# Gate and value products of a gated layer in pairs of groups and of f blocks, two of three k blocks by a scheme of seven products

## The chip, the cores and the metric

One core of a Trainium2 chip runs the whole program. Its engines run side by side, each through its own queue in order: TensorE (PE; its weight loads are listed as PEld), VectorE (DVE), ScalarE (ACT), GpSimd (POOL), and SyncE (SP), which here issues nearly all DMAs. The metric is device time in microseconds (us).

## What is computed

A delta-rule attention writes 3072 tokens x 384 features, and two feed-forward layers follow. The change is in the second, which takes the first's result `x` (3072 x 384) with 1536 hidden features (f):

```python
def _moe2_ref(x, w_gate, w_val, w_out):
    gate = 1.0 / (1.0 + np.exp(-(x @ w_gate)))
    val = x @ w_val
    return (gate * val @ w_out).astype(np.float32)
```

All is float32. A number is kept as two parts in a reduced format, a high part and the rest ("lo", the number minus its high part), and each matrix product is three: high x high, lo weight x high input, high weight x lo input.

## The kernel before

The tokens stand in six groups of 512 (`GT`, group index g), the 1536 hidden features in twelve blocks of 128 (`NF2`, index f), the 384 input features in three k blocks (`KD`). Values are laid out with features on partitions and the 512 tokens of a group in the free dimension, so a matmul is 128 x 128 weights against 128 x 512 inputs, written to one bank of PSUM (there are eight).

All instructions are recorded in the order in which they shall stand (`manual_schedule`). Attention and most of the first layer follow a table of tokens, `ORDER`; the last group of the first layer and the whole second layer are plain loops, at the end of the kernel function. In the first layer's last group (line 828) step n issues the hidden product `moe1_h`, the loads of the next weight rests from DRAM on SP (`fetch_low`), the output product `moe1_o` of step n - 2 and VectorE's rest `moe1_g`; between them stand the loads and splits of the second layer's weights (`w2_load`, `w2_split`), the making of float weights from raw 64-bit numbers (`w2_late`, steps of `narrow`) and of the first input (`load_x2`, `split_x2`).

The second layer runs over n = (g, f) from line 947. `moe2_h` makes the gate and the value sum of one block: 9 matmuls each (3 k blocks x 3 parts) into a tile `gv`, of which there are four. ScalarE takes the sigmoid of the first (`sg`), VectorE multiplies it with the second (`p`), ScalarE makes its high part (`ph`), VectorE its rest (`pl`). Then `moe2_o` of n - 1 stands on TensorE: the second product of the block before, 9 matmuls (3 output blocks x 3 parts) added up over f in three banks `o0` to `o2`. After a group's last f VectorE transposes the three banks and SP writes them out. In the last group the second product is turned round (`ph` and `pl` are the weights, 384 columns), 12 matmuls per f into four banks, and needs no transpose.

## Time and profile before

| | |
|---|---|
| median of three runs | 1099.5 us (1098.2 to 1100.1) |
| profiled execution: device time, span | 1103.99 us, 1102.3 us |
| mean granted TensorE clock | 0.98 |
| busy share of the span: PE, PEld, DVE, ACT, POOL | 93%, 78%, 53%, 39%, 14% |
| share of TensorE in the chain that ended last | 87% |

The span runs from the first to the last instruction. The busy share is a mean over very different stretches: attention and first layer up to 653 us, second layer after that. What a change in the second layer does is read there. A matmul's duration in a row is its latency; the next one starts before it has ended, so the pace is read from the distance of starts. Where an instruction sat idle before it started, the row names what ended the wait.

### The profile page before, as it was taken

The page shows a single profiled execution, that of the slowest core. Times are in us where ns is not written, and L with a number is a line of the kernel's source. Part 1 is how long each engine was busy: PE and PEld are TensorE (multiplying, and loading weights), DVE is VectorE, ACT ScalarE, POOL GpSimd, SP SyncE. Part 2 cuts the span into 40 slices and gives each one's busy share as a digit, 9 for nine tenths or more (in the row PEclk, how much of TensorE's full clock was granted, in tenths as well). Part 3 has the DMA queues.
Part 4 walks back from the last instruction along what each step waited for, and adds up shares of the span by engine and source line. Part 5 has one row for each costly group of instructions (what it writes and reads, how often), then busy time and mean ns, then how long its engine had stood idle before and what let it go on. Part 6 is the DMA issues. An engine that isn't in the chain of part 4 may idle for free.

```text
span 1102.3 us, 26935 instructions
## 1 busy us (share of the span) xinstructions
PE 1030.3 (93%) x11719; PEld 854.8 (78%) x11719; DVE 581.5 (53%) x1099; ACT 429.5 (39%) x688; POOL 150.0 (14%) x117
## 2 busy tenths in 40 slices
PE   3576999989999999999997999999999999999997
PEld 2474788878887888888885888888888888888886
DVE  6779889858777776775232357532222222322221
ACT  2253665544463555455444564312212112122111
POOL 4352454101001101010100020300001001000000
PEclk9998999999998999999997999999999999999999
DMA  9766667675774956665555652101020010010101
GB/s 242 193 208 166 214 209 203 195 189 145 211 200 144 232 159 193 184 167 174 135 169 154 202 199 94 43 20 38 1 58 1 4 55 1 20 38 1 29 1 29
DMA packets 93030, 135.56 MB, mean 123 GB/s; under 512 B 45552, under 2 KB 72304, under 8 KB 92400
## 3 DMA queue, kind: packets, MB, share of 16 engines
q1 hardware_dynamic: 92624, 133.57, 42.4%
q8 instruction: 92, 1.51, 0.6%
q10 hardware_dynamic: 288, 0.26, 0.1%
q14 instruction: 26, 0.21, 0.1%
HBM read 108.63 MB, written 20.45 MB: 117 GB/s over the span
## 4 chain that ended last, share of the span: by engine, by line
PE 87%; DVE 5%; DMA 3%; issue 3%; ACT 1%; SPq 1%; POOL 0%; DVEq 0%; ACTq 0%; POOLq 0%
PE gv L867 27%; PE h L665 17%; PE o L703 17%; PE o L893 11%; PE o L929 2%; PE att L582 2%; PE att L539 1%; PE att L524 1%; PE att L351 1%; PE att L570 1%; DMA il<-w1d 1%; PE att L552 1%; DMA kn<-in_kn_dram 1%; PE att L604 1%; DVE tt L440 1%
## 5 line engine op out<-in xcount | busy, mean ns | idle before, releaser
L875 DVE TENSOR_TENSOR p<-sg,gv 128x512 f32<-128x512 f32 x72 | 49.5, 687 | 252.9 <-PE gv L867 252.9
L679 ACT ACTIVATE gg<-h 128x512 f32<-128x512 f32 x96 | 57.4, 598 | 198.2 <-PE h L665 193.2
L688 DVE TENSOR_TENSOR gl<-gg,gh 128x512 fp32r<-128x512 f32 x96 | 72.3, 759 | 102.0 <-ACT gg L682 101.7
L867 PE MATMUL gv<-xhi,w2h 128*128 128x512 f32 x432 | 121.5, 389 | 0.0
L867 PE MATMUL gv<-xlo,w2h 128*128 128x512 f32 x432 | 121.4, 389 | 0.0
L867 PE MATMUL gv<-xhi,w2l 128*128 128x512 f32 x432 | 121.4, 389 | 0.0
L703 PE MATMUL o<-gh,il 128*128 128x512 f32 x288 | 113.2, 393 | 5.7 <-DMA il<-w1d 5.7
L873 ACT ACTIVATE sg<-gv 128x512 f32<-128x512 f32 x72 | 43.0, 597 | 172.0 <-PE gv L867 172.0
L877 ACT CAST ph<-p 128x512 fp32r<-128x512 f32 x72 | 44.6, 620 | 157.3 <-DVE p L875 157.3
L867 PEld LDWEIGHTS gv<-xlo,w2h 128*128 128x128 f32 x432 | 81.1, 188 | 17.0
L867 PEld LDWEIGHTS gv<-xhi,w2l 128*128 128x128 f32 x432 | 81.1, 188 | 17.0
L867 PEld LDWEIGHTS gv<-xhi,w2h 128*128 128x128 f32 x432 | 80.9, 188 | 16.2
L703 PE MATMUL o<-gh,w1h 128*128 128x512 f32 x216 | 87.6, 405 | 0.0
L665 PE MATMUL h<-xhi,il 128*128 128x512 f32 x288 | 84.7, 403 | 2.1 <-issue 1.7
L703 PE MATMUL o<-gl,w1h 128*128 128x512 f32 x216 | 85.1, 394 | 0.0
L879 DVE TENSOR_TENSOR pl<-p,ph 128x512 fp32r<-128x512 f32 x72 | 50.6, 703 | 49.4 <-ACT ph L877 49.4
L116 POOL TENSOR_TENSOR xlo<-x2r,xhi 128x512 fp32r<-128x512 f32 x18 | 24.7, 1370 | 335.5 <-ACT xhi L115 335.5
L893 PE MATMUL o<-ph,w2h 128*128 128x512 f32 x180 | 70.0, 389 | 0.0
L893 PE MATMUL o<-ph,w2l 128*128 128x512 f32 x180 | 70.0, 389 | 0.0
L893 PE MATMUL o<-pl,w2h 128*128 128x512 f32 x180 | 70.0, 389 | 0.0
L665 PE MATMUL h<-xhi,w1h 128*128 128x512 f32 x216 | 66.3, 417 | 1.9 <-ACT gg L679 1.9
L665 PEld LDWEIGHTS h<-xhi,il 128*128 128x128 f32 x288 | 55.9, 195 | 15.2 <-issue 2.2
(142 smaller groups left out, 1845.6 us busy)
## 6 DMA issues: line engine op xcount, KB each, us to landing
il<-w1d SPq DMA_DIRECT2D x192, 192.0 KB, 3.6
raw<-in_w_dram SPq DMA_DIRECT2D x19, 768.0 KB, 4.8
w1s<-in_w_dram SPq DMA_DIRECT2D x9, 768.0 KB, 5.1
w1d<-wl SPq DMA_DIRECT2D x16, 384.0 KB, 4.1
kz<-in_kz_dram SPq DMA_DIRECT2D x32, 192.0 KB, 5.2
kn<-in_kn_dram SPq DMA_DIRECT2D x12, 384.0 KB, 4.6
kt<-in_kq_dram SPq DMA_DIRECT2D x24, 192.0 KB, 5.2
q<-in_kq_dram SPq DMA_DIRECT2D x24, 192.0 KB, 5.2
```

The source lines that it names most:

```text
L116: eng.tensor_tensor(out=dst_lo, in0=src, in1=dst_hi.bitcast(F32), op=ALU.subtract)
L582: nc.tensor.matmul(out=psv[c][tok(a), k, :], lhsT=k2_t[st][tok(a), 8 * c + k, :], rhs=u_t[st][tok(a), 8 * c + k, 0:HD], start=True, stop=True,
L665: nc.tensor.matmul(out=ps[:, cs], lhsT=w[:, kc * 128:kc * 128 + 128], rhs=x[:, kc, cs], start=(i == 0 and kc == 0), stop=(i == 2 and kc == ...
L679: nc.scalar.activation(out=gg, in_=ps, func=ACTF.Relu)
L688: nc.vector.tensor_tensor(out=gl, in0=gg, in1=gh.bitcast(F32), op=ALU.subtract)
L703: nc.tensor.matmul(out=po[m], lhsT=w[:, cs], rhs=x, start=(f == 0 and i == 0), stop=(f == NF1 - 1 and i == 2),)
L867: nc.tensor.matmul(out=ps, lhsT=w[:, kc * 128:kc * 128 + 128], rhs=x[:, kc, :], start=(i == 0 and kc == 0), stop=(i == 2 and kc == KD - 1),)
L873: nc.scalar.activation(out=sg, in_=pss[0], func=ACTF.Sigmoid)
L875: nc.vector.tensor_tensor(out=p, in0=sg, in1=pss[1], op=ALU.mult)
L877: nc.scalar.copy(out=ph, in_=p)
L879: nc.vector.tensor_tensor(out=pl, in0=p, in1=ph.bitcast(F32), op=ALU.subtract)
L893: nc.tensor.matmul(out=po2[m], lhsT=w[:, m * 128:m * 128 + 128], rhs=x, start=(f == 0 and i == 0), stop=(f == NF2 - 1 and i == 2),)
```

## The change

The loop over (g, f) goes. Groups are taken in pairs and f blocks in pairs, so a step has four sums to make: A, B, C, D for two groups x two f blocks, first for the gate, then for the value. One such step for the gate or the value is a half in what follows; there are 36 (3 pairs of groups x 6 pairs of f blocks x 2).

Of the three k blocks, two form with the two groups and the two f blocks a product of 2 x 2 block matrices. It is made with seven block products of sums and differences of the weights (`w_sums`) and of the inputs (`x_sum`) in place of eight. The third k block takes four products as before (`K11` to `K22`). With three parts each that is 33 matmuls in a half. They stand in seven pieces (`PIECES`) of one or two block products, each piece with a PSUM bank of its own, `gx` and `gy` in turn. The first is copied by ScalarE into a tile in SBUF, every later one is added by VectorE to one or two of the tiles A to D, seven adds in a half. When a sum is complete (`DONE`) the sigmoid (gate) or the product with the gate (value) is made in place in SBUF, and then high part and rest as before.

The second product is issued in small portions between pieces (`FILL`: 3, 2, 2, 3, 2, 3 and 3 matmuls after the seven pieces), from a queue that is filled after each value half. Two groups are summed up at a time, so six banks hold the second product and two the pieces. In halves 0 and 1, where the queue is empty, and in the last nine halves, where only one group needs banks (the portions are `FILL_END` there), the pieces have five banks. The last group's second product comes at the very end, one output block of 36 matmuls after another.

Weights are made once, in the first pair of groups: ScalarE's high parts, VectorE's sums, GpSimd's rests; they are stored to DRAM (`w_keep`, 1.2 MB a half) and fetched again two halves ahead in the later pairs (`w_fetch`). Sums, high parts and rests of the inputs of the next pair are made by ScalarE and GpSimd during the pair before; those of the first pair by ScalarE and VectorE in the last group of the first layer, where the splits of before stood. Weights of the last four f blocks are made from raw numbers in twelve slabs of 384, seven in the first layer's last group and five in halves 2 to 6. Tiles of the first layer move to a pool of their own; the table `ORDER` is the same.

TensorE, in the middle of the second layer, before (`gv` the gate or value sum, `o` the second product; w2h and w2l are high part and rest of the weights):

```order
L867 MATMUL gv<-xhi,w2l_8993 128x512 x3
L867 MATMUL gv<-xlo,w2h_8992 128x512 x3
L893 MATMUL o_9601<-ph,w2h_8990 128x512 [waits Activation_49]
L893 MATMUL o_9601<-ph,w2l_8991 128x512
L893 MATMUL o_9601<-pl,w2h_8990 128x512 [waits DVE_49]
L893 MATMUL o_9602<-ph,w2h_8990 128x512
```

The same of the changed kernel (`gx` and `gy` the two banks of the pieces, `xb` input sums, `wg` weights, `wo` output weights):

```order
L1135 MATMUL gx<-xb,wg 128x512 [waits DVE_49]
L1135 MATMUL gx<-xb,wg 128x512 x5
L1014 MATMUL o_10499<-gh,wo 128x512
L1014 MATMUL o_10499<-gl,wo 128x512
L1014 MATMUL o_10472<-p_10774,wo 128x512
L1135 MATMUL gy<-xb,wg 128x512 [waits DVE_49]
L1135 MATMUL gy<-xb,wg 128x512 x2
L1014 MATMUL o_10472<-p_10774,wo 128x512
L1014 MATMUL o_10472<-p_10775,wo 128x512
```

The 9 matmuls of a second product are spread over four pieces, and nearly every piece begins with a wait for VectorE.

VectorE in the second layer before, where a group ends:

```order
L875 TENSOR_TENSOR p<-sg,gv 128x512 [waits PE_49,Activation_49]
L879 TENSOR_TENSOR pl<-p,ph 128x512 [waits Activation_49]
L901 STREAM_TRANSPOSE obt<-o_10094 128x16x32 [waits DMAHW4_49,DMAHW3_49,DMAHW5_49,DMAHW2_49,DMAHW6_49,DMAHW1_49,DMAHW7_49,DMAHW0_49,PE_49]
L901 STREAM_TRANSPOSE obt<-o_10095 128x16x32 [waits PE_49]
L901 STREAM_TRANSPOSE obt<-o_10096 128x16x32 [waits PE_49]
```

VectorE in a value half of the second pair of groups (L1047 are the adds from the piece's bank, L1058 the product with the gate, L1066 the rest):

```order
L1047 TENSOR_TENSOR valB<-valA,gx 128x512 [waits PE_49,Activation_49]
L1047 TENSOR_TENSOR valA<-valA,gy 128x512 [waits DVE_49,PE_49]
L1047 TENSOR_TENSOR valC<-valB,gx 128x512 [waits PE_49]
L1058 TENSOR_TENSOR valA<-gateA,valA 128x512 [waits DVE_49]
L1047 TENSOR_TENSOR valD<-valB,gy 128x512 [waits PE_49]
L1047 TENSOR_TENSOR valB<-valC,gy 128x512 [waits DVE_49]
L1047 TENSOR_TENSOR valC<-valC,gx 128x512 [waits DVE_49,PE_49]
L1066 TENSOR_TENSOR gl<-valA,gh 128x512 [waits Activation_49]
L1058 TENSOR_TENSOR valB<-gateB,valB 128x512
L1047 TENSOR_TENSOR valD<-valD,gy 128x512 [waits PE_49]
L1058 TENSOR_TENSOR valC<-gateC,valC 128x512 [waits DVE_49]
L1066 TENSOR_TENSOR gl<-valB,gh 128x512 [waits Activation_49]
```

Two operations per block have become eleven per half, and an add stands behind products and rests of the blocks before it.

VectorE in the first layer's last group before (gl is that layer's own rest, w2l the rest of second-layer weights):

```order
L116 TENSOR_TENSOR w2l_8492<-t,w2h_8491 128x1152 [waits DMAHW5_49,Activation_49]
L688 TENSOR_TENSOR gl<-gg,gh 128x512 [waits DVE_49,PE_49]
L688 TENSOR_TENSOR gl<-gg,gh 128x512 [waits DVE_49,PE_49,Activation_49]
L138 TENSOR_SCALAR y_8891<-raw_8786 128x1152 [waits DMAHW1_49,Activation_49]
L142 SCALAR_TENSOR_TENSOR raw_8786<-raw_8786,y_8891 128x1152 [waits DVE_49]
```

And of the changed kernel (L790 to L800 a slab, L910 and L922 sum and rest of an input, L868 rests of weights, L700 the layer's own rest):

```order
L868 TENSOR_TENSOR wg<-wr,wg 128x640 [waits Activation_49]
L700 TENSOR_TENSOR gl<-gg,gh 128x512 [waits PE_49,Activation_49]
L790 TENSOR_SCALAR y_8490<-raw_8489 128x384 [waits DMAHW5_49,DMAHW4_49,Activation_49]
L794 SCALAR_TENSOR_TENSOR raw_8489<-raw_8489,y_8490 128x384 [waits DVE_49]
L798 TENSOR_SCALAR y_8490<-raw_8489 128x384 [waits DVE_49]
L800 SCALAR_TENSOR_TENSOR raw_8489<-raw_8489,y_8490 128x384 [waits DVE_49]
L910 TENSOR_TENSOR xt<-x2r,xt 128x512
L922 TENSOR_TENSOR xlo<-x2r,xhi 128x512 [waits Activation_49]
L868 TENSOR_TENSOR wg<-wr,wg 128x512 [waits Activation_49]
```

Behind each of the layer's own rests stand seven operations here where two or three stood. The core of the diff:

```diff
-W2A, W2B = 6, 8
+W2A, W2B = 4, 8
+NP = NF2 // 2
+W_PLACE = dict(B2=0, B3=1, A1=2, A2=3, A3=4, S1=5, S2=6, S3=7, S4=8)
+X_PLACE = dict(P1=0, P6=1, P2=2, K1=3, P7=4, P5=5, P4=6, K2=7, P3=8, KD=9)
+UNITS = dict(
+    P1=("A1", "P1"), P6=("S2", "P6"), P2=("A2", "P2"), P7=("S3", "P7"), P5=("S1", "P5"), P4=("B2", "P4"),
+    P3=("S4", "P3"), K11=("A3", "K1"), K12=("A3", "K2"), K21=("B3", "KD"), K22=("B3", "K2"),
+)
+PIECES = ("P1", "P6", "P2 K11", "P7 K22", "P5", "P4 K21", "P3 K12")
+DONE = {2: ("A", 0, 1), 4: ("B", 1, 0), 5: ("C", 0, 0), 6: ("D", 1, 1)}
+FILL, FILL_END = (3, 2, 2, 3, 2, 3, 3), (2, 1, 1, 1, 1, 1, 2)
...
+        def w_sums(q):
+            t = raw_w[q]
+            b = [t[:, 128 * i:128 * i + 128] for i in range(10)]
+            for d, p, m, op in ((6, 0, 1, ALU.add), (7, 6, 3, ALU.subtract), (8, 3, 0, ALU.subtract), (9, 4, 7, ALU.subtract)):
+                nc.vector.tensor_tensor(out=b[d], in0=b[p], in1=b[m], op=op)
...
+        def w_low(q, i, eng=None):
+            a, b = (128 * x for x in PARTS[i])
+            h, t = ring_w[q][:, 0, a - 128:b - 128], ring_w[q][:, 1, a - 128:b - 128]
+            (eng or nc.vector).tensor_tensor(out=t, in0=raw_w[q][:, a:b], in1=h.bitcast(F32), op=ALU.subtract)
...
-        def moe2_h(n):
...
-            for v in range(2):
-                hi, lo = (w[:, v * DM:(v + 1) * DM] for w in w2_t[f])
-                ps = ps_2.tile([128, GT], F32, tag="gv", name="gv")
-                for i, (w, x) in enumerate([(hi, xh), (lo, xh), (hi, xl)]):
-                    for kc in range(KD):
...
+        def o_product(g, f, m, i, start, stop):
+            if start:
+                po2[g, m] = (
+                    ps_o.tile([128, GT], F32, tag=f"o{m}", name=f"o{m}") if g % 2 == 0
+                    else ps_2.tile([128, GT], F32, tag=f"o{m + 3}", name=f"o{m + 3}")
+                )
+            hi, lo = (w[:, m * 128:m * 128 + 128] for w in wo_t[f])
+            ph, pl = p_t[g, f]
+            w, x = ((hi, ph), (lo, ph), (hi, pl))[i]
+            nc.tensor.matmul(out=po2[g, m], lhsT=w, rhs=x, start=start, stop=stop)
...
+        def gate_done(t):
+            nc.scalar.activation(out=t, in_=t, func=ACTF.Sigmoid)
+        def val_done(t, sg, key):
+            nc.vector.tensor_tensor(out=t, in0=sg, in1=t, op=ALU.mult)
+            def high():
+                p_t[key] = p_tiles(key)
+                nc.scalar.copy(out=p_t[key][0], in_=t)
+            def low():
+                ph, pl = p_t[key]
+                (nc.gpsimd if key[0] in PLP else nc.vector).tensor_tensor(out=pl, in0=t, in1=ph.bitcast(F32), op=ALU.subtract)
+            later(PHD, high)
+            later(PLD, low)
...
+            if hh == 2:
+                p2.close()
+                ps_2 = ps_g = p2.enter_context(tc.tile_pool(name="ps_2", bufs=1, space=PSUM, reuse_waits="tile"))
...
+            if q < 2 * NP:
+                for k, i in enumerate((WP0, WP1)[v]):
+                    bg.setdefault(i, []).append((
+                        lambda: w_high(q, 0), lambda: w_sums(q), lambda: w_high(q, 1), lambda: w_low(q, 0, WLE[0]), lambda: w_low(q, 1, WLE[1])
+                    )[k])
...
+            for i, piece in enumerate(PIECES):
+                us = piece.split()
+                b = "xy"[step[0] % 2]
+                ps = ps_g.tile([128, GT], F32, tag=f"g{b}", name=f"g{b}", bufs=1 if 1 < hh < wide else {"x": 2, "y": 3}[b])
+                for u in us:
+                    wk, xk = UNITS[u]
+                    at_ = 128 * W_PLACE[wk]
+                    hi, lo = (w[:, h, at_:at_ + 128] for h in range(2))
+                    xh, xl = x[xk]
+                    for k, (a, c) in enumerate([(hi, xh), (lo, xh), (hi, xl)]):
                         nc.tensor.matmul(
-                            out=ps, lhsT=w[:, kc * 128:kc * 128 + 128], rhs=x[:, kc, :],
-                            start=(i == 0 and kc == 0), stop=(i == 2 and kc == KD - 1),
+                            out=ps, lhsT=a, rhs=c, start=k == 0 and u == us[0], stop=k == 2 and u == us[-1],
                         )
-                pss.append(ps)
-            sg = w2x.tile([128, GT], F32, tag="sg", name="sg")
-            nc.scalar.activation(out=sg, in_=pss[0], func=ACTF.Sigmoid)
-            p = work.tile([128, GT], F32, tag="gg", name="p")
-            nc.vector.tensor_tensor(out=p, in0=sg, in1=pss[1], op=ALU.mult)
-            ph = work.tile([128, GT], F32R, tag="gh", name="ph", bufs=3)
-            nc.scalar.copy(out=ph, in_=p)
-            pl = work.tile([128, GT], F32R, tag="gl", name="pl", bufs=3)
-            nc.vector.tensor_tensor(out=pl, in0=p, in1=ph.bitcast(F32), op=ALU.subtract)
-            p_t[n] = (ph, pl)
+                if i == 0:
+                    nc.scalar.copy(out=t["A"], in_=ps)
+                else:
+                    steps = ("BA", "AA", "CB", "DB BC", "CC", "DD")[i - 1].split()
+                    for d, a in steps:
+                        add(t[d], t[a], ps)
+                    if i in DONE:
+                        d, k, f = DONE[i]
+                        key = g0 + k, 2 * j + f
+                        if v == 0:
+                            later(GD, lambda d=t[d]: gate_done(d))
+                        else:
+                            later(VD[i], lambda d=t[d], sg=sgs[d], key=key: val_done(d, sg, key))
+                for fn in after.pop(step[0], ()):
+                    fn()
+                for fn in bg.pop(i, ()):
+                    fn()
+                for _ in range((FILL, FILL_END)[hh >= wide - 1][i]):
+                    if queue:
+                        one, end = queue.pop(0)
+                        one()
+                        if end is not None:
+                            closing(end)
+                for _ in range(3):
+                    if puts:
+                        puts.pop(0)()
+                step[0] += 1
...
+            if v:
+                assert not queue
+                for k, (g, f) in enumerate(((g0, fo), (g0, fe), (g0 + 1, fe), (g0 + 1, fo))[:4 if g0 + 2 < NG else 2]):
+                    for m in range(KD):
+                        for r in range(3):
+                            queue.append([
+                                lambda g=g, f=f, m=m, r=r, a=j == 0 and k % 2 == 0 and r == 0, z=j == NP - 1 and k % 2 and r == 2:
+                                o_product(g, f, m, r, bool(a), bool(z)), None])
+                    if j == NP - 1 and k % 2:
+                        queue[-1][1] = g
...
+        for m in range(4):
+            cs = slice(m * 128, m * 128 + 128)
+            po_m = ps_r.tile([128, DM], F32, tag=f"r{m}", name=f"r{m}")
+            for f in range(NF2):
+                hi, lo = wo_t[f]
+                ph, pl = p_t[NG - 1, f]
+                        out=po_m, lhsT=x[:, cs], rhs=w, start=f == 0 and i == 0, stop=f == NF2 - 1 and i == 2
```

## Rows read from the trace of the kernel before

**Rows 1.** Page: span, busy time with share and instructions.

```profile
span 1102.3 us, 26935 instructions
...
PE 1030.3 (93%) x11719; PEld 854.8 (78%) x11719; DVE 581.5 (53%) x1099; ACT 429.5 (39%) x688; POOL 150.0 (14%) x117
```

**Rows 2.** Windows: busy us of PE, PEld, DVE, ACT, POOL; clock, DMA, GB/s.

```profile
653.30:700.00 46.70, 46.70 (x208) 38.67 (x207) 28.22 (x31) 20.55 (x28) 7.12 (x4) 1.00 0.38 136
...
900.00:1000.00 100.00, 100.00 (x443) 82.82 (x442) 24.89 (x37) 23.05 (x39) 6.44 (x5) 1.00 0.06 16
```

**Rows 3.** Chain that ended last, in order of time: start us, us, what.

```profile
804.41 4.08 PE gv L867 x18
...
810.53 4.08 PE gv L867 x18
...
1091.08 4.28 PE o L929 x24
```

**Rows 4.** One line's instructions: duration ns min/median/max, first and last start us.

```profile
L867 PE MATMUL gv<-xhi,w2h x432: 389/389/398, 653.3 to 1089.3; 128*128 128x512 f32 x144
```

**Rows 5.** Timeline: start us, us, engine line op, idle before and what ended it.

```profile
1021.85 0.84 PE L867 MATMUL gv<-xlo,w2h 128*128 128x512 f32 x3
...
1022.80 0.69 DVE L875 TENSOR_TENSOR p<-sg,gv 128x512 f32<-128x512 f32 x1 [4.05 <-PE gv L867]
...
581.06 0.61 ACT L679 ACTIVATE gg<-h 128x512 f32<-128x512 f32 x1
...
581.72 0.96 PE L665 MATMUL h<-xhi,w1h 128*128 128x512 f32 x3 [1.85 <-ACT gg L679]
```

**Rows 6.** Three lines as in rows 4; then groups: busy us, mean ns.

```profile
L875 DVE TENSOR_TENSOR p<-sg,gv x72: 679/687/689, 657.6 to 1091.2; 128x512 f32<-128x512 f32 x72
...
L879 DVE TENSOR_TENSOR pl<-p,ph x72: 691/692/1503, 659.0 to 1092.6; 128x512 fp32r<-128x512 f32 x72
...
L591 DVE TENSOR_TENSOR state<-state,att x20: 540/547/555, 106.6 to 548.7; 128x384 f32<-128x384 f32 x20
...
L440 DVE TENSOR_TENSOR tt<-tt,tmp 128x126 f32<-128x126 f32 x4 | 1.2, 290 | 0.1
...
L151 DVE SCALAR_TENSOR_TENSOR w1s<-w1s,y 128x768 f32<-128x768 uint32 x9 | 8.6, 959 | 0.3
...
L138 DVE TENSOR_SCALAR y<-raw 128x768 uint32<-128x768 uint32 x12 | 6.6, 551 | 4.7 <-ACT raw L133 4.7
```

**Rows 7.** Timeline, VectorE alone, operations that don't wait for each other.

```profile
504.05 1.30 DVE L688 TENSOR_TENSOR gl<-gg,gh 128x512 fp32r<-128x512 f32 x2 [7.47 <-ACT gg L682]
```

**Rows 8.** Timeline, GpSimd and VectorE where they meet, then each alone.

```profile
701.51 1.37 POOL L116 TENSOR_TENSOR xlo<-x2r,xhi 128x512 fp32r<-128x512 f32 x1 [4.26 <-ACT xhi L115]
...
701.76 2.33 DVE L142 SCALAR_TENSOR_TENSOR raw<-raw,y 128x1152 uint32<-128x1152 uint32 x1
...
684.63 1.36 DVE L142 SCALAR_TENSOR_TENSOR raw<-raw,y 128x1152 uint32<-128x1152 uint32 x1
...
767.70 1.29 POOL L116 TENSOR_TENSOR xlo<-x2r,xhi 128x512 fp32r<-128x512 f32 x1 [55.52 <-ACT xhi L115]
```

**Rows 9.** Windows, a stretch of the first layer's last group.

```profile
620.00:640.00 20.00, 19.70 (x87) 15.97 (x87) 7.78 (x8) 12.51 (x20) 3.20 (x2) 1.00 0.75 258
```

**Rows 10.** Windows and timeline, the wait for weights at 585 us.

```profile
580.00:600.00 20.00, 12.59 (x38) 9.54 (x39) 6.71 (x9) 8.40 (x15) 1.47 (x1) 0.66 0.41 131
...
590.77 0.79 PE L703 MATMUL o<-gh,il 128*128 128x512 f32 x1 [5.69 <-DMA il<-w1d]
```

**Rows 11.** Timeline and DMA issues (x count, KB, us to landing) at the end.

```profile
1095.00 0.34 PE L929 MATMUL o<-w2h,pl 128*128 128x384 f32 x1
...
1095.38 0.56 DVE L938 COPY ob<-o 128x384 f32<-128x384 f32 x1 [0.49 <-PE o L929]
...
1094.29 5.04 SPq L944 DMA_DIRECT2D out_dram<-ob  x8
...
out_dram<-ob SPq DMA_DIRECT2D x8, 96.0 KB, 2.2
```

More of the change, by code (lines that the diff above doesn't have):

```diff
@@ L205, in rests @@
     def rests(f):
[L206 removed]
+        wl_t[f] = w1s.tile([128, 2 * DM], F32R, tag="wl", name="wl", bufs=1)
         nc.gpsimd.tensor_tensor(out=wl_t[f], in0=wt_t.pop(f), in1=w1h[f].bitcast(F32), op=ALU.subtract)
@@ L808 @@
[L808 to L819 removed]
+        NW, HS, SLAB, SST = 7, (2, 3, 4, 5, 6), (2, 3, 4, 6, 7, 8, 10), 4
@@ new lines, with x_high, x_low, x_steps @@
+        X_SAME = dict(P1=(0, 0), P2=(1, 0), P3=(1, 1), K1=(2, 0), K2=(2, 1))
+        def x_high(p, u):
+            if u in X_SAME:
+                k, g = X_SAME[u]
+                xt[u] = x2r_t[:, g, k]
+            nc.scalar.copy(out=x2[p][u][0], in_=xt[u])
+        def x_low(p, u, eng):
+            eng.tensor_tensor(out=x2[p][u][1], in0=xt[u], in1=x2[p][u][0].bitcast(F32), op=ALU.subtract)
+        X_ORDER = ("P5", "P1", "P6", "P2", "P4", "K1", "KD", "K2", "P7", "P3")
+        def x_steps(p, eng_s, eng_l):
+            def one(i):
+                if i == 0:
+                    open_x(p)
+                if i < len(X_ORDER) and X_ORDER[i] not in X_SAME:
+                    x_sum(X_ORDER[i], eng_s)
+                if i:
+                    x_high(p, X_ORDER[i - 1])
+                    x_low(p, X_ORDER[i - 1], eng_l)
+            return [lambda i=i: one(i) for i in range(len(X_ORDER) + 1)]
@@ L855 @@
[L855 to L866 removed]
+            for one in plan.get(n - N1 + NF1 - 2, ()):
+                one()
@@ new lines, with later, add, closing @@
+        after, queue, puts = {}, [], []
+        step = [0]
+        def later(k, fn):
+            after.setdefault(step[0] + k, []).append(fn)
+        def add(d, a, b, eng=None):
+            (eng or nc.vector).tensor_tensor(out=d, in0=a, in1=b, op=ALU.add)
+        def closing(g):
+            for m in range(KD):
+                later(1 + 2 * m, lambda m=m: turn(g, m))
+            later(6, lambda: puts.extend(put_out(g)))
+        def gate_done(t):
+            nc.scalar.activation(out=t, in_=t, func=ACTF.Sigmoid)
@@ new lines @@
+        while after:
+            k = min(after)
+            for fn in after.pop(k):
+                step[0] = k
+                fn()
+        for one, _ in queue:
+            one()
+        for m in range(KD):
+            turn(NG - 2, m)
+        puts = put_out(NG - 2)
+        p2.close()
+        ps_r = ctx.enter_context(tc.tile_pool(name="ps_r", bufs=1, space=PSUM, reuse_waits="tile"))
+        for m in range(4):
[4 more added lines that the diff above has]
+                ph, pl = p_t[NG - 1, f]
@@ new lines @@
+            ob = obt_t.rearrange("p a (b n) -> p (a b) n", b=2)[:, m]
+            o_out = ob.rearrange("p (q m i) -> p m q i", q=4, m=KD)
+            o_in = po_m.rearrange("p (m q i) -> p m q i", q=4, m=KD)
+            if m % 2:
+                nc.vector.tensor_copy(out=o_out, in_=o_in)
+            else:
+                nc.scalar.copy(out=o_out, in_=o_in)
+            for one in puts[16 * m:16 * m + 16]:
+                one()
+            s = 2 * (NG - 1) + m // 2
+            for b in range(2):
+                r0 = (2 * (m % 2) + b) * SEQ + s * C
+                nc.sync.dma_start(out=out[r0:r0 + C, :], in_=ob[64 * b:64 * b + 64])
```

367 lines of the change are left out of this document (223 added, 144 removed).

## The prediction

> **What bounds the kernel now.** I read the page first: the span is 1102.3 us and PE is busy for 93% of it [rows 1]. The windows then say where: from 653.3 us, when the second layer begins, to 1089 us TensorE has no pause at all at a granted clock of 1.00, while VectorE is busy 28.2 of the first 46.7 us and about a quarter of the time after that [rows 2]. The chain of waits there is nothing but TensorE: one f block of one group is 27 matmuls and comes round every 6.12 us, and the last 24 matmuls end the kernel [rows 3]. So a matmul of 512 columns costs 6.12 / 27 = 0.2267 us (its 389 ns in [rows 4] are its latency, not its pace), and in this stage a matmul that goes is time that goes, as long as TensorE is never kept waiting instead. Everything up to the last group of the first layer stands on every engine in the order of before, with the same waits, so the first 600 us stay.
>
> **What is removed.** Gate and value products go from 1296 matmuls (432 of each of three kinds, one of them in [rows 4]) to 1188: for two groups, two f blocks and one of gate or value ("a half" below) 33 stand where 36 stood. The second product keeps its 540 and 144. So 108 x 0.2267 = **24.5 us** go, all of it from the path.
>
> **What is added, in the steady state.** Before, a finished gate or value sum was read once, at leisure, out of four banks. Now each half has seven pieces of 3 or 6 matmuls in two banks in turn, ScalarE copies the first and VectorE adds the other six into SBUF with seven adds, and a piece can start only when the piece two before it has been read. Between pieces stand 2 or 3 matmuls of the second product (18 in a half), so a half takes 51 x 0.2267 = 11.56 us of TensorE. Prices: a read begins 0.50 us after the last matmul of a sum has begun (gate product at 1021.85 x3, the last at 1022.30, VectorE at 1022.80) [rows 5]. An add of SBUF and PSUM is of the kind of L875, 0.687 us; L591, the same form in 384 elements, never left 0.54 to 0.56 us [rows 6]. VectorE operations that don't depend on each other start 0.61 us apart (two of 512 in 1.30 us) [rows 7], dependent ones 0.72. TensorE resumes within 0.1 us of what it waited for (ScalarE ends at 581.67, TensorE starts at 581.72) [rows 5].
> Walk through a value half, time 0 at its start. Piece 3 (counted from 0) has its last matmul 24 intervals in: read from 24 x 0.2267 + 0.50 = 5.94 to 6.63; its bank is wanted by piece 5 at interval 33, 7.48. Spare 0.85. Piece 4 has two adds: 30 x 0.2267 + 0.50 = 7.30, two dependent adds to 8.71; wanted at interval 42, 9.52. Spare 0.81. The other pieces have 1.0 us or more. Over two halves VectorE has 14 adds, 4 products and 4 subtractions, 22 x 0.61 to 0.72 = 13.4 to 15.8 us against 23.1 us of TensorE. So in the second and third pair of groups I take the pieces as hidden; what covers them is the second product between pieces, and without it each would show.
>
> **What is added, in the first pair of groups.** Here weights and inputs are prepared as well. TensorE: two halves without second product (33 matmuls) and ten of 51, 576 x 0.2267 = 130.6 us. VectorE: 132 operations as above at 0.65, 86 us; 40 weight sums of 128x128 (0.29, the 128x126 row), 11.6; 12 rests of the output weights of 384 (0.55, as L591), 6.6; five slabs of late weights, each two fused operations and two shifts of 384, by the 768-element rows (0.96 and 0.55) scaled down about 1.8 together, 9.1 [rows 6]. Sum 113 us: 87%, against 66% later. Spare of 0.8 us no longer covers everything:
> - halves 0 and 1 have no second product between pieces. Half 1 wants 7 adds, 3 products, 1 subtraction, 4 sums and 2 rests, some 10 us, from VectorE in 7.5 us of TensorE, and then five banks shrink to two: 1.0 us late at half 2.
> - halves 2, 4 and 6: four sums (1.2) and a slab operation stand between the reads of piece 3 and piece 4: 5.94 + 0.69 + 1.2 + 0.56 + 1.41 = 9.8 against 9.52, with the backlog of the half before 0.5 each: 1.5.
> - halves 7 to 11: GpSimd makes the sums and rests of the next inputs there (below): 2.0.
> Later: 0.8 in the second pair for the same work of GpSimd, 0.5 for the transposes that fall on the two-bank pieces of the next group pair, and 0.7 at the end, where the last C block's rest (VectorE 12.7 us after the start of the last half, by the same walk) is wanted 12.0 us after it. The last group of the first layer: VectorE was busy 7.8 of 20 us there [rows 9]; per step of 4.08 us it now has a subtraction of 0.69, a slab of 1.8, an input sum and rest (1.3), in two steps weight sums and rests too (5.7 us in all), so it falls 2 us behind; its result is wanted two steps later. Late weights and their stores also stand on SP ahead of the first layer's weights, two steps after the work that they wait for. 1.0. What such a wait could cost is in the trace: 5.69 us once, for weights behind a store on SP [rows 10].
> Stalls: 1.0 + 1.5 + 2.0 + 0.8 + 0.5 + 0.7 + 1.0 = **7.5 us**, between 0 (every wait covered) and the rivals below. ScalarE's and GpSimd's own time, the store and reload of the prepared weights (1.2 MB a half, 102 GB/s) and SP hide: the stage moved 16 GB/s [rows 2] where the group before it moved 258 [rows 9], no ring is wanted within 11 us of its fetch, and output DMAs go three to a piece.
>
> **The end.** Before, four output blocks finish together: the last matmul starts at 1095.00, SP issues eight DMAs until 1099.33, landing takes 2.2 us, the span ends 7.3 us after that matmul [rows 11]. Now the blocks finish one after another, 36 matmuls apart. After the last one stand a copy (1095.38 + 0.56, so 0.94 after the matmul), two issues of 0.63, 2.2 of landing and the 0.8 us that remain before too: 5.2. **2.1 us** less.
>
> **Sum.** 24.5 + 2.1 - 7.5 = 19.1 us less. The profiled execution took 1103.99 us around its span of 1102.3; the three timed runs have a median of 1099.5. The difference carries over: 1099.5 - 19.1 = **1080.4 us**.
>
> **Rivals.**
> *VectorE and GpSimd hold each other up, and VectorE becomes the bound in the first pair.* GpSimd's subtraction at 701.51 took 1.37 us, and VectorE's operation of 701.76, which reads two SBUF operands, took 2.33 us where the same line takes 1.36 at 684.63: it ended 1.21 us after GpSimd, most of an operation. Subtractions of L879 range from 0.69 to 1.50, reads from PSUM (L875, L591) never move [rows 6, 8]. In the first pair GpSimd now has 20 weight rests (1.6 and 1.3 us), five slab sums (0.8) and 15 input operations (1.29), some 52 us, scaled from [rows 8]. If half of that falls on VectorE's products, rests and sums, it has 26 us more against 17.6 spare. TensorE then waits 8.4 us if all of the spare lies where it is wanted, 17 if half does, in place of the 4.5 that I counted: 1084 to 1093 us. For it: VectorE's order is dense there. Against it: 84 of its 132 operations of the steady kind are adds from PSUM, and GpSimd is free to run where TensorE and VectorE are at others. The Trainium skill, "SBUF — State Buffer", section "Who interferes with whom", states this as a rule that speaks against the change: a VectorE instruction with two SBUF inputs and a GpSimd instruction that reads SBUF exclude each other, and whoever comes second waits the other one out; the trace agrees (0.97 us more of 1.36).
> *Two banks are too few, and it gets slower.* The place is the piece boundary, 175 of them in the 25 halves that have two banks. It decides when reads end later than my walk by more than the spare of 0.8 us: then every 0.1 us costs 17.5 us, and 0.26 us eat up all of the gain. An add that takes 1.4 us in place of 0.69 (in place in SBUF, as no row of before has it in 512) would put piece 4 0.6 us over and VectorE at 24 us of work per 23.1: at least 25 x 0.6 + 18 x 1 = 33 us more, 1113 us. Against it: L591 has exactly this form and a steady time.
> *No stall at all*: 26.6 us less, 1073.
>
> **How the numbers follow.** Forecast (1075 to 1086): 0.61. Contention beyond it (1086 to 1093 and a little more): 0.22. No stalls: 0.06. Stalls that eat it up to within 0.2% (2.2 us): 0.03. Slower: 0.08. 0.2% is about what a measurement of this kernel can tell from no change. Faster 0.89, same 0.03, slower 0.08. The range leaves out the slower rival and the tips: 1073 to 1094.
>
> **What would show it.** The second layer's matmuls 108 fewer, still 0.2267 us apart; waits of TensorE on VectorE nearly all in the first 130 us of the stage, under 2 us each; GpSimd's time in that stretch near 52 us and VectorE's near 113; VectorE's adds at 0.69 us; the last DMA issue about 2 us after the last matmul. Wrong it is if waits recur at every piece of the later pairs, if a wait is long enough for the granted clock to fall (it was 0.66 in the window of the 5.69 us wait [rows 10]), or if the last group of the first layer waits for its weights.

## The result

| | before | after |
|---|---|---|
| median, runs | 1099.9 us, 8 (1096.9 to 1102.7) | 1091.1 us, 8 (1085.3 to 1094.6) |
| ratio, 95% interval | | 0.992 (0.989 to 0.994) |
| profiled execution: device time, span | 1103.99, 1102.3 us | 1089.84, 1088.1 us |
| second layer begins, last matmul begins | 653.29, 1095.00 us | 649.94, 1083.47 us |

The kernel got faster by 8.8 us, 0.8%, where 19.1 were forecast; the time is inside the range. The page and the windows of the profile after, as in [rows 1, 2] (here the second layer's first 50 us, and the steady state):

```profile
span 1088.1 us, 27387 instructions
...
PE 1013.5 (93%) x11611; PEld 830.8 (76%) x11611; DVE 765.8 (70%) x1450; ACT 462.5 (43%) x762; POOL 200.1 (18%) x157
...
649.90:700.00 50.10, 47.52 (x203) 37.48 (x203) 44.34 (x84) 23.55 (x39) 14.94 (x11) 1.00 0.74 260
900.00:1000.00 100.00, 99.69 (x430) 80.32 (x429) 70.37 (x110) 27.73 (x47) 2.01 (x2) 1.00 0.38 125
```

TensorE is granted 1.00 and is hardly ever without a matmul, as before, with VectorE at 44 of the first 50 us and 70 of 100 us later. But there are 430 matmuls in the 100 us where [rows 2] has 443, and 0.7 us of waits account for three of them. The pace itself is slower. In the timeline (start, duration, ... xcount) and in the rows of one line (minimum, median, maximum of the duration in ns):

```profile
829.66 1.57 PE L1135 MATMUL gx<-xb,wg 128*128 128x512 f32 x6
831.06 0.40 PE L1014 MATMUL o<-gh,wo 128*128 128x512 f32 x1
...
L1135 PE MATMUL gx<-xb,wg x144: 391/394/400, 792.9 to 929.0; 128*128 128x512 f32 x144
```

Six matmuls begin at 829.66 and the next at 831.06: 0.2333 us each, not 0.2267. The latency, whose median was 389 ns [rows 4], is 391 to 400. Nothing waits there; nothing but this pace and these durations shows that anything is wrong.

All 1980 and 1872 starts of the second layer's matmuls are in the traces, so the whole can be added up. A matmul of 512 columns counts 0.2267, one of 384 columns 0.1733 (the undisturbed spacings); what a spacing has over that is put under "pace" if it is below 0.03 us, and under "waits" if above:

| second layer, us | before | after | change | forecast |
|---|---|---|---|---|
| matmuls at the undisturbed pace | 440.95 | 416.47 | -24.5 | -24.5 |
| waits | 0.04 | 7.87 | +7.8 | +7.5 (1.0 of it ahead of the second layer) |
| pace | 0.72 | 9.19 | **+8.5** | 0 |
| last matmul to end of span | 7.3 | 4.6 | -2.7 | -2.1 |
| sum | | | -10.9 | -19.1 |

The profiled spans differ by 3.4 us more, since the second layer began that much earlier. Of this 0.6 us lie in the first layer's last group, which the change touches (see below); the rest is not the change. Kernels with the same order up to that group began the second layer anywhere between 641.0 and 653.3 us in the traces here, with the granted clock falling at different places (mean of 580 to 610 us: 0.77 in the kernel before, 0.92 in `dose`), and the medians' -8.8 (-12.1 to -6.2 by the interval) agrees with -10.9. So three of four terms were right to within a microsecond, and the open question is 8.5 us of pace in a stage where no engine waits for another.

The waits by the profile's own count (engine, line, releaser: us, times, longest), each shorter than 2 us (5.0 us in all; the table counts from start to start, so what follows a wait is in its 7.9):

```profile
PE gx L1135 <- DVE valC L1047: 1.6, 1, 1.6
PE gx L1135 <- DVE valB L1047: 1.2, 2, 0.6
PE gx L1135 <- DVE gateB L1047: 0.9, 2, 0.5
PE gy L1135 <- DVE valD L1047: 0.6, 1, 0.6
PE o L1014 <- DVE p L1066: 0.4, 1, 0.4
PE gy L1135 <- DVE gateD L1047: 0.3, 1, 0.3
```

### The profile page after: what moved, and what is told of

Same layout as the page of the kernel before. It is cut to its first block, busy times and chain, and to the rows that moved or that the text cites. A ratio compares the mean times of both kernels' runs of the same rounds, so it can differ in the third digit from the quotient of the medians.

```text
span 1088.1 us, 27387 instructions
## 1 busy us (share of the span) xinstructions
PE 1013.5 (93%) x11611; PEld 830.8 (76%) x11611; DVE 765.8 (70%) x1450; ACT 462.5 (43%) x762; POOL 200.1 (18%) x157
## 4 chain that ended last, share of the span: by engine, by line
PE 84%; DVE 8%; issue 4%; DMA 2%; ACT 1%; POOL 1%; SPq 1%; DVEq 0%; ACTq 0%; POOLq 0%
PE o L715 18%; PE h L677 18%; PE gx L1135 11%; PE gy L1135 11%; PE o L1014 10%; PE r L1194 2%; PE att L594 2%; PE att L536 1%; PE att L551 1%; PE att L582 1%; PE att L363 1%; PE att L616 1%; PE att L564 1%; PE att L377 1%; PE att L618 1%
## 5 line engine op out<-in xcount | busy, mean ns | idle before, releaser
L700 DVE TENSOR_TENSOR gl<-gg,gh 128x512 fp32r<-128x512 f32 x96 | 73.8, 776 | 106.6 <-ACT gg L694 106.5
L1014 PE MATMUL o<-gh,wo 128*128 128x512 f32 x270 | 93.0, 394 | 0.0
L1135 PE MATMUL gx<-xa,wg 128*128 128x512 f32 x288 | 76.7, 395 | 2.1 <-DVE valB L1047 1.2
L1135 PE MATMUL gy<-xa,wg 128*128 128x512 f32 x288 | 76.2, 393 | 0.0
L715 PEld LDWEIGHTS o<-gh,il 128*128 128x128 f32 x288 | 54.9, 191 | 17.5 <-DMA il<-w1d 6.8
L1135 PEld LDWEIGHTS gx<-xa,wg 128*128 128x128 f32 x288 | 53.6, 188 | 16.4 <-DVE gateB L1047 2.3
L1135 PEld LDWEIGHTS gy<-xa,wg 128*128 128x128 f32 x288 | 53.7, 188 | 13.0 <-DVE gateC L1047 0.4
L694 ACT ACTIVATE gg<-gg 128x512 f32<-128x512 f32 x96 | 60.7, 632 | 3.1
L693 ACT ACTIVATE gh<-gg 128x512 fp32r<-128x512 f32 x96 | 60.7, 632 | 3.1
L677 PE MATMUL h<-xlo,w1h 128*128 128x512 f32 x216 | 61.9, 396 | 0.0
L1014 PE MATMUL o<-gl,wo 128*128 128x512 f32 x135 | 53.2, 394 | 0.0
```

Source lines behind the costliest of these rows:

```text
L677: nc.tensor.matmul(out=ps[:, cs], lhsT=w[:, kc * 128:kc * 128 + 128], rhs=x[:, kc, cs], start=(i == 0 and kc == 0), stop=(i == 2 and kc == ...
L693: nc.scalar.activation(out=gh, in_=gg, func=ACTF.Square)
L694: nc.scalar.activation(out=gg, in_=gg, func=ACTF.Square)
L700: nc.vector.tensor_tensor(out=gl, in0=gg, in1=gh.bitcast(F32), op=ALU.subtract)
L715: nc.tensor.matmul(out=po[m], lhsT=w[:, cs], rhs=x, start=(f == 0 and i == 0), stop=(f == NF1 - 1 and i == 2),)
L1014: nc.tensor.matmul(out=po2[g, m], lhsT=w, rhs=x, start=start, stop=stop)
```

## The experiments

**The first theory** was the place of the operands in SBUF (A). In the kernel before, all weights and inputs of the second layer begin at multiples of 64 bytes; in the changed one the pool `w2x` (with `wg`, `wo` of blocks 0 to 3, `xa`) begins 32 bytes past one (places are the tiles' addresses in the built program). The rival (B) was traffic: the stage moves 125 to 260 GB/s where [rows 2] shows 16 in the steady state, and VectorE's work has nearly tripled. Against B stood that the spacing in the changed kernel's trace (780 to 1070 us) was the same with VectorE at work all through it as with VectorE idle, 0.2320 and 0.2327 us.

**aligned.** A pad of 32 bytes moves the pool:

```diff
                 ring_w[q] = w2x.tile([128, 2, 9 * 128], F32R, tag=f"wg{q % 3}", name="wg")
+                if q == 2:
+                    w2x.tile([128, 8], F32, name="pad2")
```

> The changed kernel with every tile of the second layer's weights and inputs moved down by 32 bytes in SBUF, so that all matmul operands begin at a multiple of 64 bytes, as in the kernel before; nothing else changes, not even the order. In the changed kernel the pool w2x (wg, wo of blocks 0 to 3, xa, the kept px) began 32 bytes past one. Theory A, place in SBUF: the 512-column matmuls of the second layer go back from 0.232 to 0.2267 us apart (but for some six after a stall); of the 9.2 us that they took over 0.2267 about 1.5 stay, the 7.9 us of waits stay, so the time falls by some 7.7 us below the changed kernel, to about 1083 us, 0.985 of before. Theory B, traffic (100 to 200 GB/s of DMA and three times VectorE's work beside the matmuls): nothing moves, 0.232 us apart, about 1091 us, 0.992 of before.

Measured: 433.51 us from the first to the last matmul, pace 8.9 us, ratio 0.986 (0.981 to 0.992). Nothing came back; as it stood, A had missed. The ratio alone would have fitted A's 0.985: the stage ahead of the second layer varies by more than the effect, so the second layer's length decides, here and below.

**before_off.** The kernel before, with its pad one step smaller:

```diff
-        w2x.tile([128, 24], F32, name="pad", bufs=1)
+        w2x.tile([128, 16], F32, name="pad", bufs=1)
```

> The kernel before with one pool moved by 32 bytes: the weights of f blocks 0 to 5 of the second layer (w2h0 to w2h5, w2l0 to w2l5) now begin 32 bytes past a multiple of 64, those of blocks 6 to 11 and all inputs stay on one. Theory A: the 918 matmuls of 512 columns on blocks 0 to 5 go from 0.2267 to about 0.2334 us apart (the mean of the changed kernel's matmuls with weights off and input on), the others stay: about 6 us slower than before, 1106 us. Theory B: no change, 1100 us, 0.2267 everywhere.

Measured: 1.008 (1.004 to 1.013) of before, second layer 447.92 us for 441.71, pace 6.9 us for 0.7. The chain that ended last (start, duration, matmuls of one f block's gate and value) shows blocks 5, 6, 7, 8 and 11 of one group and block 0 of the next:

```profile
678.46 4.20 PE gv L867 x18
...
684.76 4.11 PE gv L867 x18
...
690.97 4.10 PE gv L867 x18
...
697.11 4.08 PE gv L867 x18
...
715.47 4.08 PE gv L867 x18
...
721.60 4.20 PE gv L867 x18
```

18 matmuls take 4.20 us on the moved weights (blocks 5 and 0) and 4.08 on the others once they have settled (8 and 11), in one kernel, with the same engines, traffic and clock: 6.7 ns a matmul. B cannot do that. So the place counts, but "a multiple of 64" is the wrong rule.

**w_off** and **x_off** move only one operand of `aligned` by 32 bytes: a pad ahead of `wg`, or one behind `xa` and ahead of `xb`.

> The aligned kernel, but the three buffers of gate and value weights (wg) stay 32 bytes past a multiple of 64; all inputs and the output weights are on one. Theory A with the weights deciding: the 1188 gate and value matmuls are 0.233 us apart, 7 to 8 us over aligned, near 1090 us. Theory A with the difference between weights and input deciding gives the same. If the moving input decides: no change against aligned. Theory B: as the changed kernel, 1091 us.

> The aligned kernel, but the inputs xa and xb lie 32 bytes past a multiple of 64, and all weights on one: 864 of the 1188 gate and value matmuls read their moving operand there. If the moving operand, or a difference between the two operands, decides: these 864 are 0.230 to 0.2334 us apart, 3 to 6 us over aligned, 1086 to 1089 us. If only the weights decide: as aligned, about 1083 us. Theory B: as the changed kernel, 1091 us.

Measured: second layer 433.86 and 433.64 us, ratios 0.987 (0.982 to 0.991) and 0.989 (0.985 to 0.993). Both are within 0.4 us of `aligned`, which by A they should have exceeded by 7 to 8 and by 3 to 6 us (pace 10.0 and 9.6 us for 8.9), so `aligned` was already nearly as slow as they are. What the undisturbed kernel has and none of these has is more: all its operands begin 128 bytes past a multiple of 256. In `aligned`, `wg`, `wo` of blocks 0 to 3 and `xa` begin 192 past one and the rest 128.

**all_equal** makes the pad of `aligned` 24 elements in place of 8, so that every operand of the second layer begins at 128 of 256.

> In the run with all operands on multiples of 64 bytes nothing came back, though 32 bytes slowed the kernel before: what its operands have in common is more, they all begin 128 bytes past a multiple of 256 (in that run wg, wo and xa began at 192 of 256, the other inputs at 128). Here the pool is moved by 64 bytes more, so that every operand of the second layer begins at 128 of 256. Theory A, place in SBUF relative to the other operand: the 512-column matmuls are 0.2267 us apart but for some after each stall; of the 8.9 us over that about 1 stays, waits stay near 8, so from the first to the last matmul of the second layer 426 us in place of 433.5; time 0.981 of before, 7.5 us under the changed kernel. Theory B, traffic or the short sums: 433.5 us again, 0.992 of before.

Measured: 1078.4 us, ratio **0.982** (0.977 to 0.986), second layer 425.89 us against 426 expected, pace 0.67 us, waits 8.7. The rows that answer to those of the changed kernel above:

```profile
span 1077.8 us, 27387 instructions
...
897.00:997.00 100.00, 99.67 (x439) 81.93 (x438) 71.53 (x112) 29.45 (x50) 1.48 (x1) 1.00 0.38 124
...
824.32 1.52 PE L1137 MATMUL gx<-xb,wg 128*128 128x512 f32 x6
825.68 0.39 PE L1016 MATMUL o<-gh,wo 128*128 128x512 f32 x1
...
L1137 PE MATMUL gx<-xb,wg x144: 388/389/390, 788.5 to 921.1; 128*128 128x512 f32 x144
```

Six matmuls from 824.32 to 825.68, 0.2267 each, latency 388 to 390 ns, 439 matmuls in 100 us, with 124 GB/s beside them and VectorE as busy as in the changed kernel: B falls here for good.

**dose** takes the kernel before and gives f blocks different places, by pads between them.

```diff
+                n, d = ((0, 0), (8, 0), (8, 0), (8, 0), (8, 0), (8, 0), (0, 0), (40, 0), (0, 4), (8, 0), (8, 0), (8, 0))[f]
+                if n:
+                    pool.tile([128, n], F32, name=f"pad{f}")
```

> The kernel before, each f block's weights at another place: offset from the inputs' place modulo 256 bytes 0 (blocks 0, 6, 9), 32 (1, 10), 64 (2, 11), 96 (3), 128 (4), 160 (5, 7); block 8 has its two parts at 176 and 208. Theory A: blocks 0, 6 and 9 at 0.2267 us, those at 32, 64, 96, 160 at about 0.233; block 4 tells the grain: 0.2267 if it is 128 bytes, 0.233 if it is 256. The second layer then takes 7 to 9 us more than in the kernel before. Theory B: 0.2267 in all.

Measured: second layer 450.89 us (+9.2, a little over the 7 to 9 expected). The chain for blocks 0 to 6, and 9, of one group:

```profile
714.18 4.08 PE gv L872 x18
...
720.36 4.20 PE gv L872 x18
...
726.60 4.20 PE gv L872 x18
...
732.90 4.21 PE gv L872 x18
...
739.21 4.17 PE gv L872 x18
...
745.49 4.20 PE gv L872 x18
...
751.78 4.13 PE gv L872 x18
...
770.57 4.12 PE gv L872 x18
```

Equal places (block 0): 4.08. Off by 32, 64, 96 (1, 2, 3) and 160 (5): 4.20. Block 4, off by 128, takes 4.17, so 128 is not enough, if a little better. A whole 256 costs nothing: in the kernel before the weights begin 0, 256, 512 and 768 bytes from the inputs' place modulo 1024, and all four run at 0.2268 to 0.2270 us. Blocks 6 and 9, back in place behind a displaced block, take 4.13 and 4.12: there the spacing needs some matmuls to settle (behind block 11 it did not, as block 0 shows). That it is the difference between the operands and not the absolute place is seen in the changed kernel: in its first two halves weights and `xa` are both at 224 of 256, and there stretches of `xa` alone run at 0.2267 after one to five matmuls, until an operand at 128 (`xhi`) comes:

```profile
656.15 1.52 PE L1135 MATMUL gx<-xa,wg 128*128 128x512 f32 x6
657.51 0.63 PE L1135 MATMUL gy<-xhi,wg 128*128 128x512 f32 x2
```

**after_again**: the changed kernel once more, on the same chip as `best`, a version of `all_equal` (below).

> The changed kernel once more, on the same chip as the improved one, so that the two are compared without a change of chip: 0.991 to 0.992 of before, 433.5 us from the first to the last matmul of the second layer, 512-column matmuls 0.232 us apart; if the place in SBUF is the whole difference to all_equal, it is 0.9 to 1.2% above the improved kernel here too.

Measured: 0.990 (0.986 to 0.994), second layer 433.52 us, pace 9.12, waits 7.93: the second layer's length repeats to a hundredth, its terms to a tenth. Its median, 1086.4 us, is 0.5% above that of `best`, 1080.6, and not 0.9 to 1.2%: that part missed. The second layers differ by 8.7 us, which is 0.8%; the rest lies in the part ahead of them, which varies from run to run.

**The waits.** Of the 7.9 us, where do they come from? Two runs take work away from `all_equal`, and three try to mend it. Waits of TensorE by half, in us (half 36 is the last C blocks):

| half | forecast | after | all_equal | pool_idle | prep_out | five_banks | slab_early |
|---|---|---|---|---|---|---|---|
| 2 | 1.5 | 2.51 | 2.78 | 2.42 | 1.37 | 1.42 | 2.79 |
| 3, 5 | 0 | 1.79 | 2.00 | 1.38 | 2.62 | 3.09 | 2.11 |
| 4, 6 | 1.0 | 0.26 | 0.74 | 0 | 0 | 0.74 | 0.74 |
| 7 to 11 | 2.0 | 1.81 | 1.42 | 0 | 0 | 1.39 | 1.40 |
| 12 to 35 | 1.3 | 0.68 | 0.85 | 0.85 | 0.85 | 0.25 | 0.86 |
| 36 | 0.7 | 0.81 | 0.95 | 1.30 | 0.95 | 0.95 | 0.95 |
| first layer's last group | 1.0 | 0 | 0 | 0 | 0 | 0 | 0 |

**pool_idle**: in `w_low`, `nc.scalar.copy(out=t, in_=raw_w[q][:, a:b])` in place of GpSimd's subtraction.

> all_equal, but GpSimd makes no rests of gate and value weights in the first pair of groups (20 operations, 29.5 us of its 54.5 us there); in their place ScalarE copies the weights, so the rests are wrong numbers. VectorE's and TensorE's work is the same. If GpSimd's reads hold VectorE up and that causes the waits: VectorE's 128x128 sums go back from 0.385 to about 0.29 us, its rests of the output weights from 0.82 to 0.55, its products from 0.75 to 1.05 to 0.69; its sum in the pair falls from 119 to about 110 us, and of the 7.0 us that TensorE waits in that pair 3 or more go. If VectorE's own queue causes them: its operations shorten, but the waits stay within 1 us of 7.0.

Measured (VectorE's groups in the first pair: busy us, mean ns):

```profile
L885 DVE TENSOR_TENSOR wo<-wor,wo 128x384 fp32r<-128x384 f32 x12 | 6.6, 551 | 1.6 <-ACT wo L881 1.6
...
L1071 DVE TENSOR_TENSOR p<-valD,p 128x512 fp32r<-128x512 f32 x5 | 4.1, 810 | 0.0
```

Second layer 422.80 us; the first pair's waits fall from 6.9 to 3.8. The output rests took 822 ns in the changed kernel and take 551 now, the rests `p` fall from 1322 to 810, and VectorE's first pair from 118.5 to 110.9 us. The waits of halves 4 and 6 to 11 are gone. So contention with GpSimd's weight rests accounts for some 3.1 us of waits; ScalarE's 10.8 us more did not undo that. The Trainium skill, "SBUF — State Buffer", section "Who interferes with whom", says that a VectorE instruction with two SBUF inputs and a GpSimd instruction that reads SBUF exclude each other; the 822 to 551 agree. The mean of the weight sums stayed at 382 ns and that of the products `valB` at 1050, which the expectation had falling to 290 and 690: that part missed. But GpSimd causes these too, by the work that this run leaves it, its sums for the late slabs (L805) and its input operations. The 40 sums (minimum, median, maximum ns) and one meeting in the timeline:

```profile
L855 DVE TENSOR_TENSOR wr<-wr x40: 277/284/1379, 652.3 to 749.4; 128x128 f32<-128x128 f32 x40
...
677.03 1.34 DVE L855 TENSOR_TENSOR wr<-wr 128x128 f32<-128x128 f32 x3
...
677.19 0.83 POOL L805 TENSOR_TENSOR y<-raw 128x384 f32<-128x384 f32 x1 [32.92 <-DVE raw L800]
```

34 of the 40 take 277 to 294 ns; each of the six others, 448 to 1379 ns, ran while GpSimd was at work, and so did the two long ones of the six `valB` products, 1.78 us for 0.69.

**prep_out**: VectorE's weight sums and output rests of the first pair are left out; ScalarE makes copies in their place.

> all_equal, but VectorE makes neither the weight sums nor the rests of the output weights in the first pair (40 and 12 operations, 23.7 us); ScalarE copies something of the size in their place, so these weights are wrong numbers. GpSimd's work stays. If the preparation in VectorE's queue between two reads causes the waits, as the forecast has it: those at the start of half 2 (1.95 us) fall to 0.5 or less, and those later in the pair (5.0 us) to 1 or less; together 5.5 us less. If contention with GpSimd causes them: at most the halves with GpSimd's work on inputs (7 to 11) and one or two others keep theirs, 3 us or more in all stay.

Measured: second layer 422.65 us, waits of the first pair 4.0 for 6.9. At the start of half 2 the wait falls from 1.95 to 0.37 and later in halves 4 and 6 to 11 to nothing, as expected; but halves 3 and 5 got worse, 2.62 for 2.00, with less work on VectorE. In all 2.9 us went of the 5.5 expected, and the 4.0 that stay do not stand where the expectation had the contention's, so neither branch fits. As `pool_idle` and `prep_out` both clear halves 4 and 6 to 11, what the two take away can't be added up: taking away either one clears those waits. The timeline of `all_equal` says what half 3 waits for:

```profile
679.99 0.55 ACT L788 ACTIVATE raw<-raw 128x384 f32<-128x384 f32 x1
...
680.57 0.66 DVE L790 TENSOR_SCALAR y<-raw 128x384 uint32<-128x384 uint32 x1 [1.76 <-ACT raw L788]
...
681.15 0.68 DVE L1049 TENSOR_TENSOR valB<-valA,gx 128x512 f32<-128x512 f32 x1
...
681.88 0.98 PE L1137 MATMUL gx<-xa,wg 128*128 128x512 f32 x3 [0.72 <-DVE valB L1049]
```

VectorE's next operation (L790, on a late weight slab) waits 1.76 us for ScalarE, which has two long copies ahead of the slab's step; the add that frees the bank (L1049) stands behind it and starts at 681.15, though its sum was ready some 0.2 us into the pause (the piece's last matmul began at 678.50, and a read can begin 0.50 us after that [rows 5]). In `prep_out` ScalarE has yet more to do, 70.5 us in the first pair for 60.0.

**slab_early** puts the slab's ScalarE step one piece earlier and VectorE's later:

```diff
-        OP, SP0, SP1 = (1, 3), (-4, 0, 1, 3, 5, 6, 6, 9), (-4, 0, 0, 1, 3, 5, 6, 9)
+        OP, SP0, SP1 = (1, 3), (-4, 0, 1, 3, 5, 6, 6, 9), (-4, -1, 1, 2, 3, 5, 6, 9)
```

> all_equal, with one table of steps changed: in halves 3 and 5 the late weight slab's ScalarE step stands one piece before the half instead of in its first piece, and VectorE's steps on it follow one piece later than before. In all_equal VectorE stood idle for 1.76 us before 680.57, waiting with the slab's first operation for ScalarE (raw, L788), while the add that TensorE needs stood behind it; TensorE then waited 0.89. If that queueing behind ScalarE is the cause in halves 3 and 5: their waits fall from 1.0 us each to 0.3 or less, the second layer from 425.9 to about 424.5. If VectorE's own work in these halves is too long: they stay at 1.0 each.

Measured: second layer 425.85 us, halves 3 and 5 2.11 us. The expectation missed, though its mechanism did what it says:

```profile
678.54 0.54 ACT L788 ACTIVATE raw<-raw 128x384 f32<-128x384 f32 x1
...
681.71 0.69 DVE L1049 TENSOR_TENSOR valB<-valA,gx 128x512 f32<-128x512 f32 x1 [0.17 <-PE gx L1137]
...
682.15 3.14 POOL L870 TENSOR_TENSOR wg<-wr,wg 128x640 fp32r<-128x640 f32 x2 [1.16 <-ACT wg L865]
...
682.84 1.30 DVE L882 TENSOR_TENSOR wo<-wor,wo 128x384 fp32r<-128x384 f32 x1 [0.44 <-ACT wo L878]
...
684.05 1.45 DVE L790 TENSOR_SCALAR y<-raw 128x384 uint32<-128x384 uint32 x1
...
685.42 0.67 DVE L1049 TENSOR_TENSOR valA<-valA,gy 128x512 f32<-128x512 f32 x1
...
686.15 0.96 PE L1137 MATMUL gy<-xa,wg 128*128 128x512 f32 x3 [0.24 <-DVE valA L1049]
```

ScalarE's step ends before the half, the add of 681.71 is on time, and the wait of 0.89 us is gone. The next one took its place: now VectorE's output rest and slab operation fall into GpSimd's 3.14 us (1.30 and 1.45 us, for 0.55 and 0.66), the add behind them starts at 685.42, and TensorE waits 0.51 there and 0.50 two pieces later.

**five_banks** keeps the five banks of halves 0 and 1 through half 2 (`if hh == 3` in place of 2).

> all_equal, with the five piece banks kept through half 2 and the two banks from half 3 (the o sums of the odd group begin only in half 3). Half 2 has the second product between its pieces, so VectorE can catch up before the banks get fewer. If the stall of 1.95 us at the start of half 2 is the handover of a late VectorE from five banks to two, it goes, and so does the one of 0.65 us in half 2, and half 3 starts with 0.5 or less: 2 to 2.6 us less than all_equal, second layer 423.5 us, time near 1076. If VectorE's backlog lasts, the stall moves to the start of half 3 whole and the second layer stays at 426 us.

Measured: second layer 424.77 us, ratio 0.982 (0.978 to 0.985). The handover's 1.95 us go from the start of half 2, but 1.42 stand in half 2 for another reason and 1.0 at the start of half 3, seen in the waits:

```profile
PE o L1016 <- DVE gl L1068: 1.1, 1, 1.1
...
PE gy L1137 <- DVE gateD L1049: 0.7, 1, 0.7
```

The first row is the second product waiting for the rest `gl` of its input, late in the same queue. Of the 2 to 2.6 us expected in this stretch 0.3 came; half 27's 0.60 went too, which I had not expected and did not follow up. **best** joins `five_banks` and `slab_early`.

> all_equal with five piece banks through half 2 and the slab's ScalarE step early: the waits of halves 2 to 5 fall from 5.1 to about 2.5 us, the second layer from 425.9 to 423 us, the time to about 1075.5, 0.979 of before. If the stalls only move: as all_equal, 0.982.

Measured: second layer 424.85 us, 1080.6 us, ratio 0.983 (0.980 to 0.986): no better than `all_equal`. The stalls only move. What beats both the kernel before and the changed one is the pad.

## Why the prediction was wrong, point by point

- **"In this stage a matmul that goes is time that goes", 24.5 us**: right, 24.48, at the undisturbed pace.
- **"Still 0.2267 us apart"**: this step failed, and it alone makes the miss. I read the price of a matmul from a kernel whose operands all lie at one place modulo 256 bytes, and carried it to tiles that the change lays elsewhere: +8.5 us over 1728 matmuls. I looked for what could make TensorE wait and for nothing that could make it slower while it doesn't. `all_equal`, which differs by a pad alone, is 0.982 of before where the forecast is 0.983.
- **Stalls of 7.5 us**: 7.9 measured from start to start (5.0 by the profile's own count), but the sum is better than its parts, so that it came out is in part luck. The start of half 2 cost 1.87 where I had 1.0, the rest of halves 2, 4 and 6 0.9 for 1.5, halves 7 to 11 1.8 for 2.0. Halves 3 and 5 cost 1.8 that I had not named, since I took ScalarE as hidden and VectorE's queue stands behind it. The second pair's 0.8 and the transposes' 0.5 nearly vanished (0.08), while the return to five banks at half 27 cost 0.60. The last block's rest was 0.8 for 0.7.
- **The first layer's last group, 1.0**: no wait. From its matmul 216 back to its end it took 48.96 us against 49.56 before, with VectorE busy twice as long as in [rows 9]:

```profile
616.60:636.60 20.00, 20.00 (x90) 16.55 (x89) 15.73 (x30) 14.49 (x27) 4.20 (x4) 1.00 0.71 221
```

- **Prices of VectorE**: the adds take the 0.69 us of [rows 6], and the steady walk held, with no wait at all in halves 12 to 25. For the first pair VectorE had 119.3 us where I had 113 and GpSimd 54.5 for 52. The difference is in weight sums of 0.385 us for 0.29, output rests of 0.82 for 0.55, rests `p` of 1.32 for 0.65 and products `valB` of 1.05 for 0.65. These are means: 34 of the 40 sums took the 0.29 forecast, and the six longer ones, up to 1.68 us, ran beside GpSimd. So the price of a sum was right for VectorE alone; what the 113 left out is the contention, which the forecast had only as 2.0 and 0.8 us of waits (the first three rows: busy us, mean ns; the last: minimum, median, maximum ns):

```profile
L855 DVE TENSOR_TENSOR wr<-wr 128x128 f32<-128x128 f32 x40 | 13.8, 385 | 0.3
L880 DVE TENSOR_TENSOR wo<-wor,wo 128x384 fp32r<-128x384 f32 x12 | 9.9, 822 | 1.7 <-ACT wo L876 1.7
L1066 DVE TENSOR_TENSOR p<-valD,p 128x512 fp32r<-128x512 f32 x5 | 6.6, 1322 | 0.0
...
L1047 DVE TENSOR_TENSOR gateD<-gateB,gx x18: 679/689/689, 655.8 to 1040.3; 128x512 f32<-128x512 f32 x18
```

- **The end, 2.1 us less**: 2.7. After the last matmul's start at 1083.47 come the copy, two issues in 1.11 us and the landing; the span ends 4.6 us after it, 5.2 forecast:

```profile
1082.78 1.03 PE L1194 MATMUL r<-wo,px 128*128 128x384 f32 x5
...
1083.85 0.56 DVE L1201 COPY obt<-r 128x384 f32<-128x384 f32 x1 [12.03 <-PE r L1194]
1084.43 1.11 SPq L1209 DMA_DIRECT2D out_dram<-obt  x2
```

- **The rivals**: contention is real. Over the undisturbed durations of the same operations VectorE's recorded time in the first pair is some 16 us longer (an estimate from the trace's durations), all of it in operations during which GpSimd ran, where the rival had 26. TensorE's waits there came to 6.4 us, not the 8.4 to 17 of the rival, and by `pool_idle` the weight rests alone cause some 3.1 of 6.9. Two banks were enough. The measured time lies in the range that the contention rival gave, 1084 to 1093, by another cause.

## What to carry to other kernels

A matmul's pace measured in one kernel belongs to that kernel's tile addresses: when a change makes new pools, work out where each matmul operand begins and keep weights and inputs at the same place modulo 256 bytes, or try a pad. This is shown for 512-column matmuls in the reduced format of this kernel; others were not tried. When TensorE shows no waits and is still late, count matmuls per window or the starts within a run of equal matmuls, since busy share and granted clock don't show it. And taking one wait from a queue that is 85% full (119.3 of 139.7 us) lets the next one through: price the queue, not the wait.
